# A new order for the first nine units of an attention and mixture-of-experts kernel

## The chip, the core and the metric

The kernel runs on one core of a Trainium2 chip, as one program. The metric is its time on the device in microseconds. The median of three runs of the kernel before is 1054.12 us (1052.29 to 1057.37).

## The reference

Attention over 8 batches and 12 heads, 448 tokens, 64 channels, in float32: q and k are normalized by the root of their mean square (and scaled by a gain for each channel), scores = q k^T / 8, softmax over the keys, times v. The heads of a token are put side by side to x (3584 tokens of 768). Then a mixture of eight experts: logits = x w_gate + a bias that depends on the token's modality; the expert with the largest logit takes the token, and the output is its softmax weight times relu(x w1) w2, with 768, 1024 and 768 channels.

## The kernel before, in words

Attention goes by units, 48 in all: a unit is two heads of one batch. A unit has seven steps (7 x 128 = 2 x 448 rows), so unit u starts at step n = 7u. At each step the program issues, in this order, `st` (the transposed scores of step j, lines 1009 to 1022, two products in a bank of their own, and ScalarE's exponential), then what the plan has for this step of the other stages, for units further ahead or behind.

What a unit goes through:

- `load` (line 826): q and k from HBM, one of six buffers each.
- `sumsq` (834): squares on ScalarE, summed over 64 channels by VectorE, or by GpSimd for the units that the plan's entry `ps` names.
- `rstd` (866): the roots, two activations (Ln, Exp) on ScalarE and five small instructions on GpSimd, for one to three units together.
- `norm` (884): q or k times its root, on GpSimd, for the very first q on VectorE.
- `tr` (898): four transposes on TensorE into a bank, then casts: `a0` the rounded part (`xw`), `a1` and `a2` its two halves into `w1w`, `dve` the rest that rounding left, a subtraction on VectorE. Moves by DMA from SP's queue put halves on the other partitions.
- `sa` (977): the scores once more, with rows as partitions, only for their maxima; VectorE takes the maximum of each row (`at_hlw<-sa`). Two banks alternate.
- `mt` (996): a transpose of the seven columns of maxima, a copy on ScalarE and a DMA that puts them as one row (row 64) below the rest of q. The second product of `st` reads this row, so that the exponential gets scores less their maximum. For units 0 and 1 ScalarE issues this DMA itself.
- `st`, then `csum` (sums of the exponentials, GpSimd and VectorE), `av` (1048: attention times v, one bank for all units), `avcopy` (1065: copies the bank out, on ScalarE, as x transposed), `sums`, `gates`, `recips`, `xt`.

The order is written out by hand. The table `PLAN` (line 34) has offsets from 7u for the steady part and, under `first`, a step for each stage of the first units; `when` (1382) reads it. Steps from -22 to -1 are the ramp before the first score product. Each engine works through its own queue in the order of issue. `warm` (1330) issues filling products on TensorE, two instructions a call, as many as the plan's `warm` says for a step, and `warmn` more at each step below 0. Casts, copies and subtractions go into lists for later steps (`pre` for ScalarE and VectorE, `post`). From step 30 on the plan is the steady one but for a few entries. Routing runs in gaps of the attention; the experts' two products (`ph`, `py`) follow from about 550 us on.

Of the kernel before, what the change touches and what calls it, by code (L numbers as in the profile page):

```python
# [66 lines left out]
def kernel(  # L67
# [737 lines left out]
    if True:  # L805
# [92 lines left out]
        def tr(u, g):  # L898
# [66 lines left out]
            if nm == "k" and not own:  # L965
                at(pre["V"], state["n"] + 2, across)
# [29 lines left out]
        def mt(u):  # L996
            t = T[u]
            ps = ps_t.tile([128, 512], F32, tag="t", name=f"mt{u}")
# [416 lines left out]
        for n in range(P["start"], NJ * NU):  # L1415
# [309 lines left out]
```

## Time and profile before

| | us |
|---|---|
| median of three runs | 1054.12 |
| the profiled execution | 1054.4 |
| its span | 1052.6 |
| first score product of unit 0 | 27.78 |
| of unit 8 | 119.34 |

Share of busy time over the span: TensorE 97%, VectorE 71%, ScalarE 68%, GpSimd 68%. Times in the rows below count from the start of the span. A row of a timeline has start, duration, engine, line, operation, what is written and read, and in brackets how long the engine was idle before and what ended that. Most operations carry line 52 or 53, a helper's, so tiles tell them apart: `at_hlw<-sa` is a maximum of rows, `xrw<-r` a square or a norm, `xw<-tr` a first cast, `w1w<-tr,xw` and `xw<-tr,gs,xw` the subtractions, `at_hhw<-av` a copy of x.

### The profile page before, as it was taken

What the parts mean: (1) busy time and instruction counts of PE and PEld (TensorE: products, weight loads), DVE (VectorE), ACT (ScalarE), POOL (GpSimd) and SP (SyncE); (2) the same over time, 40 slices, a digit from 0 to 9 for tenths busy, and PEclk for the clock granted to TensorE, in tenths of its full rate; (3) what the DMA queues carried; (4) which work ended last, traced back from release to release, by engine and by line L of the source; (5) the groups of instructions that cost most, each with busy time, mean ns of one, the idle gap of its engine ahead of it and who ended that gap; (6) DMA issues with size and microseconds to landing.
All of it is one profiled execution on the core that took longest, in us unless ns stands there. A gap on an engine that the chain in (4) does not pass through costs nothing.

```text
span 1052.6 us, 18833 instructions
## 1 busy us (share of the span) xinstructions
PE 1025.4 (97%) x6444; PEld 816.7 (78%) x6444; DVE 742.7 (71%) x1252; ACT 714.9 (68%) x1389; POOL 715.2 (68%) x752
## 2 busy tenths in 40 slices
PE   8899999999999999999999999999999999999996
PEld 7655656666566565655658999999999999999995
DVE  6666788878888878787676886756675567556740
ACT  6887998889898898987764655545564555545531
POOL 7788777897788887788966646865545554565451
PEclk9899999999999999999999999999999999999998
DMA  7756666867677766765566605233372432234161
GB/s 193 177 126 151 148 148 163 191 156 163 133 189 162 155 158 138 180 130 125 146 205 248 136 16 166 76 106 120 115 287 81 120 106 78 78 103 121 60 210 66
DMA packets 147961, 148.21 MB, mean 141 GB/s; under 512 B 72762, under 2 KB 137742, under 8 KB 147344
## 3 DMA queue, kind: packets, MB, share of 16 engines
q1 hardware_dynamic: 122458, 105.08, 41.3%
q0 software_dynamic: 25328, 41.82, 12.4%
q8 instruction: 53, 0.87, 0.4%
q14 instruction: 52, 0.43, 0.2%
q10 hardware_dynamic: 70, 0.02, 0.0%
HBM read 150.31 MB, written 33.39 MB: 175 GB/s over the span
## 4 chain that ended last, share of the span: by engine, by line
PE 84%; DVE 5%; DMA 3%; POOL 3%; ACT 2%; issue 2%; ACTq 0%; SPq 0%; POOLq 0%; DVEq 0%
PE ph L606 23%; PE py L636 21%; PE st L1016 12%; PE av L1058 9%; PE sa L988 4%; PE tr L906 3%; PE av L1054 2%; PE xt L1121 2%; PE sm L1077 2%; DVE at_hlw L52 2%; DMA w1w<-xw 1%; PE warm L1332 1%; PE sm L1084 1%; PE sa L983 1%; POOL r2w L52 1%
## 5 line engine op out<-in xcount | busy, mean ns | idle before, releaser
L606 PE MATMUL ph<-xw,w1w 128*128 128x256 f32 x2016 | 246.5, 283 | 2.2 <-ACT at_w2lw L52 1.1
L606 PEld LDWEIGHTS ph<-xw,w1w 128*128 128x128 f32 x2016 | 244.0, 192 | 4.2 <-ACT at_w2lw L52 1.2
L52 DVE TENSOR_REDUCE at_hlw<-sa 128x1 f32<-128x448 f32 x336 | 205.7, 619 | 43.5 <-PE sa L988 21.6
L1016 PE MATMUL st<-w1w 128*128 128x448 f32 (+1 forms) x480 | 183.2, 431 | 1.7 <-ACT r2w L52 1.1
L52 POOL DMA_INDIRECT r<-in_moe_w_dram,tb_w x60 | 82.7, 1379 | 53.0 <-DVE w1w L52 37.4
L52 ACT ACTIVATE r2w<-st 128x448 f32<-128x448 f32 x168 | 91.0, 545 | 36.8 <-PE st L1016 27.6
L52 ACT ACTIVATE hhw<-ph 128x512 fp32r<-128x512 f32 x56 | 33.5, 598 | 120.7 <-PE ph L606 120.7
L52 POOL TENSOR_TENSOR r2w<-r2w 128x448 f32<-128x448 f32 (+1 forms) x72 | 83.7, 1162 | 44.7 <-DVE r2w L52 26.5
L636 PE MATMUL py<-w2lw,hhw 128*128 128x384 f32 x448 | 113.7, 334 | 0.0
L988 PE MATMUL sa<-w1w 128*128 128x448 f32 (+1 forms) x288 | 109.2, 380 | 4.4 <-DVE at_hlw L52 2.6
L1016 PEld LDWEIGHTS st<-w1w 128*128 128x128 f32 (+1 forms) x480 | 85.9, 191 | 34.8 <-ACT r2w L52 8.5
L52 DVE TENSOR_TENSOR w1w<-r,w1w 128x768 fp32r<-128x768 f32 x112 | 103.2, 950 | 11.4 <-ACT w1w L52 10.2
L52 POOL DMA_INDIRECT r2w<-in_moe_w_dram,tb_vi x48 | 49.6, 1034 | 87.3 <-DVE w2lw L52 78.6
L52 ACT CAST w1w<-xw 64x448 fp32r<-64x448 f32 x188 | 105.7, 562 | 3.6 <-issue 1.4
L52 DVE TENSOR_TENSOR w2lw<-r2w,w2ha 128x1536 fp32r<-128x1536 f32 x28 | 49.1, 1757 | 81.6 <-ACT w2ha L52 81.6
L1016 PE MATMUL st<-w1w,w2ha 65*128 65x448 f32 x288 | 101.3, 372 | 0.0
L52 POOL TENSOR_TENSOR xrw<-r,at_hlw 112x512 f32<-112x512 f32 x95 | 97.7, 1049 | 1.0 <-PE tr L906 0.4
L52 ACT ACTIVATE at_w2lw<-st 128x448 f32<-128x448 f32 x168 | 90.6, 546 | 9.3 <-PE st L1016 4.5
L52 ACT CAST w1w<-r 128x768 fp32r<-128x768 f32 x112 | 95.1, 903 | 0.1
L52 ACT ACTIVATE yw<-py,ltn 128x384 f32<-128x384 f32 x55 | 29.4, 580 | 79.1 <-PE py L636 75.6
L636 PEld LDWEIGHTS py<-w2lw,hhw 128*128 128x128 f32 x448 | 80.9, 188 | 0.0
L52 POOL TENSOR_TENSOR r2w<-r2w,at_w2lw 64x448 f32<-64x448 f32 (+1 forms) x48 | 55.2, 1150 | 19.0 <-DVE r2w L52 9.2
(298 smaller groups left out, 2210.1 us busy)
## 6 DMA issues: line engine op xcount, KB each, us to landing
w1w<-xw SPq DMA_DIRECT2D x216, 112.0 KB
xg<-xrw SPq DMA_DIRECT2D x14, 768.0 KB
xrw<-xg SPq DMA_DIRECT2D x56, 192.0 KB
r<-in_q_dram SPq DMA_DIRECT2D x19, 448.0 KB
r<-in_k_dram SPq DMA_DIRECT2D x19, 448.0 KB
w2ha<-xw SPq DMA_DIRECT2D x72, 112.0 KB
w1w<-w1w SPq DMA_DIRECT2D x48, 112.0 KB
r2w<-in_v_dram SPq DMA_DIRECT2D x24, 224.0 KB
```

The costliest lines, as they stand in the source:

```text
L52: return fn(*a, **kw)
L606: PE.matmul(ps[:, i], lhsT=lt_, rhs=rt_[:, c], start=n == 0, stop=n == 17)
L636: PE.matmul(ps[n][:, :384], lhsT=lt_[:, j, 128 * t : 128 * t + 128], rhs=rt_[:, 384 * n : 384 * n + 384], start=j == 0 and m == 0, stop=j ...
L906: PE.transpose(sp[:, c], src[:, c], idn[:CP, :CP])
L983: PE.matmul(ps[:, :S], lhsT=qm_b[u % 2], rhs=hi_b[u % 2][1], start=True, stop=True)
L988: PE.matmul(ps[:, :S], lhsT=t["qq"][r, h, a : a + 128], rhs=t["kk"][h][r], start=True, stop=True)
L1016: PE.matmul(ps[:, :S], lhsT=l, rhs=t["qq"][:, h] if first else t["ql"][0:65, h], start=first and (j != 3 or h == 0), stop=not first and (j ...
L1054: PE.matmul(t["av"][:, :S], lhsT=vd_b[u % 2], rhs=t["p"][:, 3], start=False, stop=True)
L1058: PE.matmul(t["av"][64 * h : 64 * h + 64, :S], lhsT=vv[:, u % 3, j], rhs=t["p"][:, j], start=c == 0, stop=False)
L1077: PE.matmul(R[g][32 * i : 32 * i + 32, :S], lhsT=sel[:, m], rhs=T[u + i // 2]["cs"][:, i % 2], start=m == 0, stop=False, tile_position=(0, ...
L1084: PE.matmul(sm[32 * i : 32 * i + 32, :S], lhsT=wg[:, (4 * g + i) % NP], rhs=T[4 * g + i]["xt"], start=False, stop=True, tile_position=(0, ...
L1121: PE.transpose(ps[:CP, 128 * c : 128 * c + 128], T[u]["xt"][:, c * CP : (c + 1) * CP], idn)
```

## The change

- `PLAN` gets new steps for the first units. Ahead of step 0 remain units 0 and 1 up to their transposes (unit 1's `sa` not), the squares of unit 2 and 3, and unit 2's norms. Unit 1's `sa` go into steps 1 to 4 and its `mt` into 5; unit 2's `sa` into 6 to 10, `mt` 11; unit 3's into 11 to 16, `mt` 17; `sas` lists these steps one by one. Squares, norms and transposes of units 3 to 8 come later than before.
- The roots of the first units are taken one unit at a time (`rs` with `rs0`): units 0, 1, 2, 3 each by itself, then 4 and 5 together; before it was 0, then 1 and 2, then 3 to 5.
- Filling products: 12 and not 19 calls at the first step; other counts behind it, and now also at steps 0 to 7.
- The order of the casts is a table (`casts`), by default as before; for units 0 and 1 they are spread over more steps.
- GpSimd sums the squares of two transfers only; the q of units 2 and 3 goes to VectorE.
- The transpose of unit 0's maxima uses a bank of `st` in place of one of the transposes'.
- `avcopy` is a copy by VectorE for units 0 to 7.
- The gains are loaded behind two units and not three, and multiplied after the first norm; loads of units 6 to 10 and of the first v have other steps.

```diff
-'first': {... ('sq', 2): -18, ('sk', 2): -18, ('nk', 1): -16, ('nq', 1): -13, ... ('sa', 1): -5, ('mt', 0): -8, ('tk', 2): -8, ('tq', 2): -3, ... ('tq', 3): 5, ('mt', 1): 2, ... ('mt', 2): 8, ... ('sa', 2): 1, ('sa', 3): 9, ('sa', 4): 16, ('tq', 4): 12 ...}
-'rs0': {0: 0, 2: 1, 5: 0, 7: 0, 8: 2}, 'sastep': 1
-'warm': {-22: 19, -21: 3, -20: 1, -16: 4, -15: 1, -13: 5, -10: 2, -7: 3, -6: 1, -5: 1, 5: 1, 7: 1}
-'ps': [(6, 1), (4, 0), (3, 0), (2, 0)]
+'first': {... ('sk', 2): -18, ('sq', 2): -9, ... ('nk', 1): -17, ('nq', 1): -16, ... ('mt', 0): -8, ... ('tk', 2): 2, ('tq', 2): 3, ('mt', 1): 5, ('mt', 2): 11, ... ('tk', 3): 7, ('tq', 3): 9, ('mt', 3): 17, ... ('tq', 4): 15, ('sa', 4): 17 ...}
+'rs0': {0: 0, 1: 1, 2: 2, 3: 0, 5: 1, 7: 0, 8: 2}
+'warm': {-22: 12, -21: 3, -20: 1, -16: 5, -14: 1, -12: 1, -7: 3, -6: 2, -5: 1, -4: 1, -3: 1, 0: 2, 1: 2, 2: 1, 3: 1, 4: 2, 5: 2, 6: 2, 7: 1}
+'ps': [(6, 1), (4, 0)]
+'sas': {1: (1, 1, 2, 2, 3, 3, 4), 2: (6, 7, 8, 8, 9, 9, 10), 3: (11, 12, 13, 14, 15, 15, 16)}
+'casts': {(0, 1): (3, 4, 1, 4), (0, 0): (5, 5, 1, 4), (1, 1): (1, 5, 1, 2), (1, 0): (1, 4, 4, 5)}, 'vcopy': 8
...
-            ps = ps_t.tile([128, 512], F32, tag="t", name=f"mt{u}")
+            ps = (ps_t if u else ps_s).tile([128, 512], F32, tag="t" if u else "s", name=f"mt{u}")
...
-            A.copy(t["xt"], t["av"][:, :S])
+            if u < PLAN["vcopy"]:
+                V.tensor_copy(out=t["xt"], in_=t["av"][:, :S])
+            else:
+                A.copy(t["xt"], t["av"][:, :S])
...
-        for u in range(3):
+        for u in range(2):
             load(u)
         load_gains()
...
-                if a[0] < P["early"]:
-                    at(pre["A"], n + 1, a1)
-                    at(pre["A"], n + 1, a2)
-                    at(pre["A"], n + P["late0"], a0)
-                    at(pre["V"], n + P["late0"], d_)
-                    continue
-                at(pre["A"], n + 1, a0)
-                at(pre["V"], n + 1, d_)
-                at(post, n + 1, a1)
-                at(pre["A"], n + 2, a2)
+                c = P["casts"].get(a, CASTS)
+                at(pre["A"], n + c[0], a0)
+                at(pre["V"], n + c[1], d_)
+                at(pre["A"] if a[0] < P["early"] else post, n + c[2], a1)
+                at(pre["A"], n + c[3], a2)
```

## Rows read from the trace of the kernel before

**Rows 1.** The page, busy time of each engine over the whole span:

```profile
PE 1025.4 (97%) x6444; PEld 816.7 (78%) x6444; DVE 742.7 (71%) x1252; ACT 714.9 (68%) x1389; POOL 715.2 (68%) x752
```

**Rows 2.** Busy time by stretch: width, engines, granted clock, DMA share, GB/s:

```profile
27.78:39.51 11.73, 10.11 (x40) 7.94 (x39) 7.15 (x12) 8.28 (x19) 9.62 (x12) 0.71 0.73 178
39.51:49.68 10.17, 9.25 (x48) 5.67 (x47) 7.36 (x12) 9.71 (x24) 7.28 (x11) 1.00 0.60 149
49.68:85.88 36.20, 32.05 (x157) 18.11 (x155) 23.79 (x40) 30.65 (x75) 30.72 (x56) 1.00 0.67 152
85.88:119.34 33.46, 32.42 (x168) 19.43 (x169) 24.96 (x46) 28.51 (x67) 26.66 (x29) 1.00 0.55 123
119.34:205.96 86.62, 85.82 (x466) 52.75 (x465) 70.32 (x140) 77.09 (x178) 67.91 (x74) 1.00 0.70 164
28.60:31.50 2.90, 1.77 (x9) 1.08 (x8) 2.71 (x5) 2.83 (x7) 2.82 (x4) 1.00 0.87 219
31.50:38.30 6.80, 6.30 (x18) 5.40 (x19) 3.63 (x7) 3.50 (x9) 5.32 (x6) 0.50 0.77 176
```

**Rows 3.** Timeline of the ramp, single instructions and runs of one kind:

```profile
1.50 9.42 PE L1332 MATMUL warm<-idn,ones 128*128 128x128 f32 x56 [1.50 <-POOL idn masks.py:199]
8.00 1.04 POOL L52 TENSOR_TENSOR xrw<-r,at_hlw 112x512 f32<-112x512 f32 x1
...
19.93 2.31 POOL L52 TENSOR_TENSOR xrw<-xrw 112x256 f32<-112x256 f32 x5
...
23.32 0.28 PE L999 MATMUL mt<-idn,at_hlw 128*7 128x128 f32 x1 [0.20 <-DVE at_hlw L52]
23.43 1.73 PE L1332 MATMUL warm<-idn,ones 128*128 128x128 f32 x14
...
24.54 1.32 ACTq L52 DMA_DIRECT2D w1w<-xw  x1
...
28.18 0.44 PE L1016 MATMUL st<-w1w,w2ha 65*128 65x448 f32 x1
```

**Rows 4.** VectorE's groups from 15.5 to 23.3 us, by form:

```profile
L52 DVE TENSOR_REDUCE at_hlw<-sa 128x1 f32<-128x448 f32 x7 | 4.0, 613 | 0.0
L52 DVE TENSOR_REDUCE at_hlw<-xrw 112x8 f32<-112x512 f32 x3 | 2.0, 679 | 0.0
L52 DVE TENSOR_TENSOR w1w<-tr,xw 128x448 fp32r<-128x448 f32 x2 | 1.2, 618 | 0.4 <-ACT xw L52 0.4
```

**Rows 5.** The chain of waits, 27.8 to 32.0 us: start, duration, what:

```profile
27.84 0.54 ACT xw L52
...
28.61 3.15 DMA w1w<-xw
...
32.00 0.71 PE sa L988
```

**Rows 6.** TensorE's waits from 27.7 to 119.4 us: total, times, longest:

```profile
PE mt L999 <- DVE at_hlw L52: 1.8, 3, 0.9
PE av L1058 <- ACT at_hhw L52: 1.6, 2, 0.9
...
PE sm L1077 <- POOL at_hhw L52: 1.1, 1, 1.1
```

**Rows 7.** ScalarE's groups by form: units 8 to 15, then 26 to 28 us:

```profile
L52 ACT CAST w1w<-xw 64x448 fp32r<-64x448 f32 x32 | 18.0, 562 | 0.4
L52 ACT ACTIVATE at_w2lw<-st 128x448 f32<-128x448 f32 x29 | 15.8, 546 | 1.2 <-PE st L1016 0.5
...
L52 ACT ACTIVATE xrw<-r 112x512 f32<-112x512 f32 x17 | 10.7, 631 | 0.2
L52 ACT ACTIVATE xw<-tr,gs 128x448 fp32r<-128x448 f32 x8 | 5.1, 632 | 0.0
...
L52 ACT COPY at_hhw<-av 128x448 f32<-128x448 f32 x3 | 1.5, 516 | 0.0
L53 ACT ACTIVATE at_hlw<-at_hlw,lnb 112x48 f32<-112x48 f32 x2 | 0.7, 334 | 0.1
```

More of the change, by code (lines that the diff above doesn't have):

```diff
@@ new lines @@
+PLAN = {'rtj': 6, 'rushat': 36, 'av': (1, 1, 4, 6), 'xt': 4, 'xte': (2, 5), 'sm': 2, 'la': 6, 'rc': 9, 'csv': (1,), 'csj': (3, 6), 'csd': (1, 1), 'cse': (2, 1), 'sa': 14, 'mt': 6, 'tk': 21, 'tq': 18, 'nq': 26, 'nk': 26, 'sk': 49, 'sq': 50, 'rs': 48, 'ld': 58, 'first': {('sq', 0): -22, ('sk', 0): -21, ('nk', 0): -20, ('nq', 0): -18, ('sq', 1): -19, ('sk', 1): -19, ('sk', 2): -18, ('sq', 2): -9, ('rs', 0): -20, ('rs', 1): -18, ('rs', 2): -7, ('tk', 0): -18, ('tq', 0): -17, ('nk', 1): -17, ('nq', 1): -16, ('tk', 1): -13, ('tq', 1): -11, ('sa', 0): -15, ('mt', 0): -8, ('nk', 2): -5, ('nq', 2): -3, ('tk', 2): 2, ('tq', 2): 3, ('mt', 1): 5, ('mt', 2): 11, ('sk', 3): -6, ('sq', 3): -4, ('rs', 3): 1, ('nk', 3): 3, ('nq', 3): 3, ('tk', 3): 7, ('tq', 3): 9, ('mt', 3): 17, ('sk', 4): 2, ('sq', 4): 3, ('sk', 5): 5, ('sq', 5): 6, ('rs', 5): 8, ('nk', 4): 10, ('nq', 4): 11, ('tk', 4): 13, ('tq', 4): 15, ('sa', 4): 17, ('mt', 4): 24, ('nk', 5): 13, ('nq', 5): 14, ('tk', 5): 18, ('tq', 5): 21, ('sa', 5): 24, ('mt', 5): 31, ('sk', 6): 9, ('sq', 6): 10, ('sk', 7): 13, ('sq', 7): 14, ('rs', 7): 17, ('nk', 6): 19, ('nq', 6): 20, ('tk', 6): 23, ('tq', 6): 25, ('sa', 6): 30, ('mt', 6): 37, ('nk', 7): 23, ('nq', 7): 25, ('tk', 7): 29, ('tq', 7): 31, ('sa', 7): 37, ('mt', 7): 45, ('sk', 8): 16, ('sq', 8): 18, ('rs', 8): 30, ('nq', 8): 35, ('mt', 8): 50, ('sk', 9): 24, ('sq', 9): 23, ('nq', 9): 31, ('tk', 9): 43, ('ld', 6): -6, ('ld', 7): -4, ('ld', 8): 0, ('ld', 9): 6, ('ld', 10): 16}, 'rs0': {0: 0, 1: 1, 2: 2, 3: 0, 5: 1, 7: 0, 8: 2}, 'start': -22, 'warm': {-22: 12, -21: 3, -20: 1, -16: 5, -14: 1, -12: 1, -7: 3, -6: 2, -5: 1, -4: 1, -3: 1, 0: 2, 1: 2, 2: 1, 3: 1, 4: 2, 5: 2, 6: 2, 7: 1}, 'warmn': 1, 'early': 1, 'pmp0': 2, 'ramp': 10, 'pmp': (0, 0, 1, 1, 1, 0, 1), 'nv': [(0, 0)], 'pmpa': (1, 0, 1, 0, 1, 1, 1), 'rush': (1, 1, 1), 'ps': [(6, 1), (4, 0)], 'pa': [], 'rtr': 6, 'sml': 4, 'lv': (-4, 0), 'lg': 16, 'lz': 13, 'gc': 24, 's1': (1, 4), 'sas': {1: (1, 1, 2, 2, 3, 3, 4), 2: (6, 7, 8, 8, 9, 9, 10), 3: (11, 12, 13, 14, 15, 15, 16)}, 'casts': {(0, 1): (3, 4, 1, 4), (0, 0): (5, 5, 1, 4), (1, 1): (1, 5, 1, 2), (1, 0): (1, 4, 4, 5)}, 'vcopy': 8}
@@ L35 @@
+CASTS = (1, 1, 1, 2)
 MANUAL = {ET.PE, ET.DVE, ET.Activation, ET.Pool, ET.SP}
@@ L965, in tr @@
             if nm == "k" and not own:
-                at(pre["V"], state["n"] + 2, across)
+                at(pre["V"], state["n"] + 1 + PLAN["casts"].get((u, g), CASTS)[1], across)
             return a0, a1, a2, dve
@@ L1335 @@
         A.preload_act_table_set("natural_log_exp_and_others")
-        for u in range(3):
+        for u in range(2):
             load(u)
         load_gains()
-        for u in range(3, 6):
+        for u in range(2, 6):
             load(u)
@@ L1482 @@
                 norm(*a, V if a in P["nv"] else G)
-                if a == (0, 0):
+                if a == (0, 1):
                     gain_product()
```

5 lines of the change are left out of this document (2 added, 3 removed).

## The prediction

> **What bounds the kernel now.** The page first: TensorE is busy for 1025.4 of 1052.6 us, 97% [rows 1], so what can still be won lies in stretches where it waits or multiplies for nothing. Then the busy time by stretch, cut at the first score product (line 1016) of a unit, seven steps to a unit [rows 2]. Units 8 to 15 take 86.62 us, 10.83 each, with TensorE busy for 85.82: there TensorE itself is the limit, and nothing in this change reaches them. Ahead of them lie 27.78 us before the first score product and 91.56 us for units 0 to 7 (11.73 + 10.17 + 36.20 + 33.46). In these eight units TensorE is busy for 83.8 us, ScalarE for 77.2 and GpSimd for 74.3, so they are limited by waits that go round between engines, and one row shows the clock granted at half, 0.50 from 31.5 to 38.3, after a stretch with TensorE busy for 1.77 of 2.90. What unit 8 starts earlier, all behind it starts earlier: the order from step 30 on is the same in both plans, and I carry a gain at unit 8 one to one to the end.
>
> **The start: 5.1 us earlier.** Filling products stand ahead of the first transposes: 56 instructions to 10.92, 168 ns each; GpSimd's first product, the normalized k, was ready at 9.04 [rows 3]. The new plan puts 42 there (seven calls of two instructions fewer), which end at 8.57, so the transposes start at about 9.15 and the first `sa` product at about 12.0, behind twelve more filling instructions at 124 ns (1.73 / 14) [rows 3]. Then VectorE decides: from 15.5 to 23.3 it does unit 0's seven row maxima (613 ns each) and, between them, three sums of squares (2.0 us) and subtractions, unit 1's among them [rows 4]. The squares of units 2 to 5 move behind and the roots of unit 1 no longer wait for unit 2's, so from the first to the last maximum only the seven (4.3) and unit 0's two subtractions (about 0.62 each) are left: 5.5 us from 12.6, and unit 0's row transpose (line 999) runs at about 18.3 and not 23.32. Another bank costs it nothing: it waited for VectorE, not for a bank; the bank keeps it from queueing behind unit 1's casts, which are now late. The gains' loads, now ahead of unit 2's on SP, and the other steps of v's and later loads I cost at nothing: the first norms and squares read units 0 and 1 alone, and unit 1's moves are not read until step 1. A load that waits on SP for the norm that frees its buffer would delay the moves behind it; that is in the bounds of the two waits below. From its copy's issue at 24.54 to the product that reads the row at 28.18 were 3.6 us [rows 3]; from an issue at 18.85 that makes 22.45. Filling behind the transpose is now 34 instructions (4.2 us), so the first score product comes at 22.7: -5.1. If VectorE's early work hides no more than the filling taken away, it is -2.4; were the row alone the limit, -5.4.
>
> **Unit 0: 2.6 us longer.** What was done before the first score product is now inside unit 0: all of unit 1's `sa` products (steps 1 to 4), unit 2's transposes (steps 2, 3), three squares, one root. ScalarE is the queue in which this stands. Behind the first row's copy and its issue (1.32 us of ScalarE's time [rows 3]) come the rest of unit 1's casts (about 1.6), a root's two activations (0.7) and two squares (0.63 each): free at about 23.6. From there to the copy of unit 1's row: six exponentials (546 ns), a root (0.7), three squares (1.9) and unit 2's casts (0.63 + 4 x 0.56 + 0.54 and two small ones, 3.9) [rows 5, 7]: 9.8 us, issue at 33.6, row there at 37.2. TensorE reaches unit 1 at about 33.9 (11.2 us for unit 0, ScalarE's pace) and waits 3 us, because the row's transpose stands two steps ahead of its reader, where before it stood five. Queued behind that product are all of TensorE's work, and ScalarE's exponentials behind it. So unit 0 takes 14.3 and not 11.73. Bounds: no wait (11.2, 0.5 less than before) and 3.5 more than before, if loads hold up the row's DMA too.
>
> **Unit 1: 2.6 us longer.** Unit 3's `sa` starts two steps behind unit 3's q transpose (steps 9 and 11); before there were four. The chain of waits shows what lies between: the cast at 27.84 (0.54), a move of 3.15 us to its landing, 0.24 to the product at 32.00 [rows 5], 4.2 us in all. In two steps TensorE has some 1.5 us of work of its own. Counted from unit 1's row, q's transpose ends 4.7 behind (the first eight products of `av` stand ahead of it), ScalarE is some 0.7 late, and 4.2 make 9.6; TensorE is at the product by 6.2. I take a wait of 2.6, below the difference of 3.4, since the 3.15 was measured with the DMA engines 0.87 busy and unit 1 of before had 0.60 [rows 2]; unit 1's row transpose for unit 2 stands behind the same product. TensorE's own work behind the row is about 10.1, a steady unit's 10.7 [rows 2] with one transpose and two `sa` more and without sums, gates and x: 12.7 with the wait, and not 10.17. Bounds of the wait: nothing and 3.4.
>
> The Trainium skill (DMA: Bandwidth & Descriptors, Anatomy of one DMA) puts the fixed cost of a DMA at about 2.0 us, most of it the receipt of the last write. By that both waits would be some 1.1 us shorter, an estimate from that page, and the sum 2.2 better; the move's 3.15 [rows 5] is what this kernel pays, so the row decides.
>
> **Units 2 to 4: 0.8 shorter.** Here the eight copies of x count. On ScalarE one is 516 ns [rows 7]; on VectorE no row shows it: between 0.52 (the same) and 0.68 (its slowest reduction of 512 columns [rows 4]); I take 0.61, its reduction of 448 columns from the same memory. ScalarE loses 0.5 a unit, VectorE gains 0.6, and what stands behind it there are the maxima that free the `sa` buffers. TensorE waited 1.6 us in all for that copy, the single bank of `av` being free only then, 1.8 for row maxima and 1.1 for GpSimd's sums [rows 6]. The first goes. GpSimd is relieved of two sums of squares (2.31 each [rows 3]; 0.68 each on VectorE) and gets two more roots, so its 1.1 goes by half. But unit 4's `sa` again starts two steps behind its transpose (about 1.7 of wait), and ScalarE gets five squares more (3.2), unit 2's k casts (1.8) and two roots (1.4) and loses 3.6 of copies: 80 us of work in the eight units. So 35.4 and not 36.2; bounds 34 (ScalarE without a wait) and 37.5.
>
> **Units 5 to 7: 0.9 shorter**, the copies' wait alone: 32.5; bounds 31.9 and 33.5.
>
> **The sum.** -5.1 + 2.6 + 2.6 - 0.8 - 0.9 = -1.6 us. The profiled execution took 1054.4 (span 1052.6), 0.3 above the median of 1054.1, so against either it is the same step: 1052.5.
>
> **Rivals.** (1) *The two waits don't come*, because ScalarE, not the landing, sets TensorE's pace at both places: unit 0 11.2, unit 1 10.2, the rest as above: 22.7 + 11.2 + 10.2 + 35.4 + 32.5 = 112.0 for unit 8, 7.3 earlier: 1047. For it: in units 2 to 4 ScalarE is busy for 30.65 of 36.20 [rows 2], and more lands on it. Against it: the gap that a move needs, 4.2 us, is more than two of TensorE's steps.
> (2) *Slower: the clock falls in the wait for unit 1's row and again in that for unit 3's move.* Place: behind steps 7 and 11. It decides if TensorE's share there is no better than the 61% after which the clock fell in the kernel before [rows 2]; filling of one or two calls stands in each of steps 0 to 7 against it, none behind. Price: in 6.8 us at half clock TensorE was busy for 6.3, so 3.1 of full-clock work is lost each time: one fall 1055.6, two 1058.7. That the clock is released by activity and held back without it is also what the Trainium skill says (TensorE: Matmul & The Clock Gate, Part 1); the trace agrees, with 0.50 in that stretch.
> (3) *VectorE becomes the wait*: copies and two more sums of squares (6.3 us) land between maxima, and the later row transposes wait for it as unit 0's did. Then units 2 to 7 gain nothing and lose about 1: 1055. For it: 1.8 us of such waits already [rows 6]; against it: it is busy for 23.79 of 36.20.
>
> **How the numbers follow.** Forecast 0.38 (1049.5 to 1055.5), first rival 0.36, second 0.15, third 0.11. About 0.5%, 5.3 us, is what a measurement of this kernel can tell from no change: below 1048.8 lie most of the first rival (0.32) and 0.05 of the forecast, 0.37; above 1059.4 the worse half of the second and a little of the third, 0.12; between them 0.51. The range of 8 in 10 reaches over the first rival down to 1043.5 (its units 2 to 7 at their lower bounds, 2.0 less, and its start) and to two falls of the clock: 1059.
>
> **What would show it.** Right: the first score product at about 22.7, the row transpose ahead of it at 18.3; ScalarE without idle time in unit 0; TensorE idle for some 3 us ahead of unit 1's second product until a DMA of the ACT queue lands, and again ahead of the first `sa` product of unit 3; no wait of `av` for a copy; unit 8 at about 117.7. Wrong: a first score product later than 25; unit 1 started by 35 (then the first rival); a granted clock of 0.50 behind either wait; `av` or row transposes waiting for VectorE more than 2 us in all; any difference of stages behind unit 8.

## The result and the profile after

The changed kernel takes 1066.2 us (median of six runs, 1062.9 to 1067.7), the kernel before in the same comparison 1054.6 (1052.3 to 1057.4): 1.011 times as long, 95% interval 1.009 to 1.0129. The forecast was 1052.5 with 1059.0 as its upper end. The profiled execution took 1066.56 us with a span of 1064.8. Line numbers of the changed kernel are one higher than before in the rows below, those of the filling products (1336) four higher.

The page after, busy time of each engine, to be set beside [rows 1]:

```profile
PE 1030.3 (97%) x6448; PEld 817.5 (77%) x6448; DVE 749.2 (70%) x1262; ACT 712.4 (67%) x1385; POOL 708.0 (66%) x750
```

No engine does noticeably more. The stretches after, cut as before at the first score product of a unit (unit 0; unit 1; units 2 to 4; 5 to 7; 8 to 15), then one stretch ahead of a fall of the clock and three at half clock, in the columns of [rows 2]:

```profile
23.10:36.14 13.04, 9.86 (x58) 7.49 (x57) 7.68 (x13) 11.31 (x27) 11.13 (x22) 1.00 0.81 205
36.14:55.20 19.06, 15.09 (x56) 9.04 (x54) 9.99 (x16) 11.33 (x25) 11.58 (x20) 0.73 0.41 105
55.20:95.97 40.77, 34.77 (x163) 19.03 (x161) 28.71 (x48) 31.73 (x77) 31.02 (x57) 0.96 0.61 136
95.97:128.94 32.97, 32.48 (x169) 19.46 (x169) 26.11 (x49) 27.43 (x64) 26.20 (x28) 1.00 0.53 126
128.94:215.56 86.62, 85.81 (x466) 52.79 (x465) 71.22 (x142) 76.43 (x176) 67.84 (x74) 1.00 0.73 164
33.00:37.78 4.78, 2.01 (x11) 1.35 (x11) 2.61 (x5) 3.42 (x9) 3.34 (x7) 1.00 0.73 185
37.78:44.61 6.83, 6.33 (x18) 3.26 (x18) 2.62 (x5) 3.27 (x7) 2.97 (x6) 0.50 0.45 110
51.44:54.85 3.41, 3.41 (x9) 2.29 (x8) 1.82 (x3) 1.98 (x4) 3.41 (x5) 0.50 0.32 93
71.92:75.33 3.41, 3.41 (x13) 1.75 (x13) 2.33 (x4) 3.15 (x8) 3.33 (x4) 0.50 0.52 106
```

Set against the terms of the forecast, in us (difference from before):

| | forecast | profiled |
|---|---|---|
| start | -5.1 | -4.7 (23.10) |
| unit 0 | +2.6 | +1.3 (13.04) |
| unit 1 | +2.6 | +8.9 (19.06) |
| units 2 to 4 | -0.8 | +4.6 (40.77) |
| units 5 to 7 | -0.9 | -0.5 (32.97) |
| unit 8's first score product | -1.6 | +9.6 (128.94) |

By this cut the wait for unit 1's row, which the forecast counted with unit 0 (some 3 of its 14.3 us), lies in unit 1, behind that unit's first product.

Units 8 to 15 take 86.62 as before, so what is lost at unit 8 is not won back there. The span is 12.2 longer; the 2.6 that are not in these 9.6 lie behind unit 15, most of them (2.1) in the stretch from unit 47 to the last `ph`. It takes 478.5 us before, 480.6 after, and between 477.7 and 480.6 in the experiments, whatever they change in the first units, so I don't count it as the change's.

Every instant of TensorE up to unit 8's first score product can be sorted, from its records, into its own work at full clock, filling products, what the work took longer at half clock (half of its time there), and idle time (us; where two records overlap, the later one counts):

| kernel | work | filling | lost to half clock | idle | sum |
|---|---|---|---|---|---|
| before | 87.2 | 18.4 | 3.0 | 10.7 | 119.3 |
| changed | 88.0 | 18.6 | 6.6 | 15.7 | 128.9 |

So the 9.6 are 5.0 of idle time and 3.6 of slow clock, and 1.0 of work and filling.

TensorE's waits after, 23 to 129 us: total, times, longest (before: [rows 6]):

```profile
PE st L1017 <- DMA w1w<-xw: 3.8, 2, 2.1
PE sa L989 <- DMA w1w<-xw: 3.5, 2, 2.3
PE sa L989 <- DVE at_hlw L53: 2.6, 3, 1.9
```

Most of this is waiting for what a DMA brings: 3.8 for rows of maxima and 3.5 for moved halves, where before there was one such wait, 0.50 at 32.00. The wait of attention's bank for the copy of x is gone. The four waits of units 0 and 1, for unit 1's maxima, for the move that unit 2's first `sa` product reads, for unit 1's row and for the move that unit 3's first `sa` product reads:

```profile
33.40 0.28 PE L1000 MATMUL mt<-idn,at_hlw 128*7 128x128 f32 x1 [1.11 <-DVE at_hlw L53]
35.72 0.44 PE L989 MATMUL sa<-w1w 128*128 128x448 f32 x1 [1.19 <-DMA w1w<-xw]
38.28 0.74 PE L1017 MATMUL st<-w1w,w2ha 65*128 65x448 f32 x1 [1.69 <-DMA w1w<-xw]
49.91 0.44 PE L989 MATMUL sa<-w1w 128*128 128x448 f32 x1 [2.28 <-DMA w1w<-xw]
```

The chain of waits tells what they wait for:

```profile
35.27 0.15 ACT xw L53
35.45 2.79 DMA w1w<-xw
...
47.60 2.17 DMA w1w<-xw
...
54.20 0.92 DVE r2w L53
...
55.21 0.95 issue
```

First the row of unit 1 (its copy ends at 35.42, its DMA takes 2.79, unit 1's second product starts at 38.28), then the move for unit 3's first `sa` product (49.91), then VectorE's queue for unit 3's sixth (from 54.20). Unit 3's own row is the fourth place. SP's queue shows why:

```profile
63.60 1.35 SPq L141 DMA_DIRECT2D wg<-in_moe_w_gate_dram  x2
65.00 0.61 SPq L143 DMA_DIRECT2D modr<-in_moe_modality_id_dram  x1
65.65 0.55 SPq L144 DMA_DIRECT2D bia<-n_moe_modality_bias_dram  x1
66.25 0.43 SPq L832 DMA_DIRECT2D r<-in_k_dram  x1
66.77 0.81 SPq L1005 DMA_DIRECT2D w1w<-xw  x1
```

Unit 3's transposed maxima left TensorE at 64.8, but four loads of the gates' tables (`lg`, step 16) and a load of k (step 17) stand ahead of the row on SP; it is issued at 66.77, and its reader starts at 71.17 after a wait of 2.15.

The ramp after (before: [rows 3]):

```profile
1.49 7.60 PE L1336 MATMUL warm<-idn,ones 128*128 128x128 f32 x42 [1.49 <-POOL idn masks.py:199]
...
19.28 0.28 PE L1000 MATMUL mt<-idn,at_hlw 128*7 128x128 f32 x1 [0.27 <-DVE at_hlw L53]
...
19.83 3.51 PE L1336 MATMUL warm<-idn,ones 128*128 128x128 f32 x30
23.10 0.45 PE L1017 MATMUL st<-w1w 128*128 128x448 f32 x1
```

### The profile page after: what moved, and what is told of

Read it like the earlier page. It is cut to its first block, busy times and chain, and to the rows that moved or that the text cites. A ratio compares the mean times of both kernels' runs of the same rounds, so it can differ in the third digit from the quotient of the medians.

```text
span 1064.8 us, 18847 instructions
## 1 busy us (share of the span) xinstructions
PE 1030.3 (97%) x6448; PEld 817.5 (77%) x6448; DVE 749.2 (70%) x1262; ACT 712.4 (67%) x1385; POOL 708.0 (66%) x750
## 4 chain that ended last, share of the span: by engine, by line
PE 78%; DVE 9%; ACT 4%; DMA 3%; issue 3%; POOL 1%; SPq 1%; ACTq 0%; POOLq 0%; DVEq 0%
PE ph L607 19%; PE py L637 19%; PE st L1017 12%; PE av L1059 10%; PE sa L989 5%; PE tr L907 3%; PE av L1055 2%; PE xt L1125 2%; DVE at_hlw L53 2%; PE sm L1081 2%; DMA w1w<-xw 1%; DVE w1w L53 1%; DVE w2lw L53 1%; PE sa L984 1%; DVE yw L53 1%
## 5 line engine op out<-in xcount | busy, mean ns | idle before, releaser
L53 DVE TENSOR_TENSOR w1w<-r,w1w 128x768 fp32r<-128x768 f32 x112 | 103.3, 953 | 11.3 <-ACT w1w L53 10.1
L53 ACT ACTIVATE at_w2lw<-st 128x448 f32<-128x448 f32 x168 | 90.8, 544 | 17.9 <-PE st L1017 12.0
L53 POOL TENSOR_TENSOR xrw<-r,at_hlw 112x512 f32<-112x512 f32 x95 | 97.6, 1047 | 0.6
L989 PEld LDWEIGHTS sa<-w1w 128*128 128x128 f32 (+1 forms) x288 | 55.3, 192 | 19.5 <-DVE at_hlw L53 7.1
```

The costliest lines, as they stand in the source:

```text
L53: return fn(*a, **kw)
L989: PE.matmul(ps[:, :S], lhsT=t["qq"][r, h, a : a + 128], rhs=t["kk"][h][r], start=True, stop=True)
```

## The experiments

All ratios are to the kernel before, run beside them. "Units" gives the lengths of units 0 to 4, in us, from the profiled execution (before: 11.7, 10.2, 12.0, 11.2, 13.0; changed: 13.0, 19.1, 13.1, 14.6, 13.0).

**1. Filling ahead of the four products that waited** (the changed kernel).

```diff
+FILL = {('sa', 2, 0): 4, ('st', 1, 0): 6, ('sa', 3, 0): 9, ('st', 3, 0): 8}
+def fill(ps, *what):
+    for _ in range(FILL.get(what, 0)):
+        PE.matmul(ps[:, :128], lhsT=ones, rhs=idn, start=True, stop=True)
```

> The changed kernel with filling products put into four of the places where TensorE waits: 4 ahead of unit 2's first sa product, 6 ahead of unit 1's first score product, 9 ahead of unit 3's first sa product, 8 ahead of unit 3's first score product. They go to the bank that the product behind them overwrites. Theory A (the clock): the changed kernel lost its time because the granted clock fell three times (0.50 from 37.8 to 44.6, 51.4 to 54.9 and 71.9 to 75.3), half of the 13.2 us that TensorE was busy there; the waits themselves are the smaller part. Then the clock stays at 1.00, unit 1 shrinks from 19.1 to about 13.5 and unit 3 from 14.6 to about 13, and the time is about 6 us below the changed kernel, 1060. Theory B (the waits and ScalarE's pace alone; the falls lie on top of waits): less than 2 us gained, 1064 to 1067, even where the clock stays up.

Measured: 1064.8 us, 1.0105 (1.0088 to 1.0122): the time is theory B's, the length of unit 1 theory A's. Units 14.4, 13.2, 18.2, 11.1, 15.7. Units 1 and 2, the first two rows of a view by stretch:

```profile
37.50:50.71 13.21, 12.57 (x73) 8.87 (x72) 8.03 (x14) 10.03 (x23) 9.69 (x17) 1.00 0.40 98
50.71:68.94 18.23, 14.30 (x74) 8.36 (x73) 12.50 (x18) 11.89 (x28) 11.17 (x16) 0.91 0.56 133
```

Unit 1 falls from 19.06 to 13.21 at a clock of 1.00, while unit 0, which holds ten of the filling products, grows from 13.04 to 14.38: 4.5 us less for both, close to the 4.9 that TensorE lost in unit 1 to half clock. But the loss turns up again, in units 2 and 4, where the clock now falls (55.4 and 89.6). VectorE and GpSimd in unit 2 of this kernel:

```profile
50.39 3.00 DVE L53 SCALAR_TENSOR_TENSOR r2w<-at_w2lw,half 128x448 f32<-128x448 f32 x1
53.32 0.61 DVE L53 COPY at_hhw<-av 128x448 f32<-128x448 f32 x1
53.85 0.67 DVE L53 SCALAR_TENSOR_TENSOR xw<-tr,gs,xw 128x448 fp32r<-128x448 f32 x1
54.44 0.67 DVE L53 TENSOR_REDUCE at_hlw<-xrw 112x8 f32<-112x512 f32 x1
55.04 0.61 DVE L53 TENSOR_REDUCE at_hlw<-sa 128x1 f32<-128x448 f32 x1
...
49.77 1.04 POOL L53 TENSOR_TENSOR xrw<-r,at_hlw 112x512 f32<-112x512 f32 x1
50.77 1.15 POOL L53 TENSOR_TENSOR at_w2lw<-r2w,at_w2lw 128x448 f32<-128x448 f32 x1
51.88 1.03 POOL L53 TENSOR_TENSOR xrw<-r,at_hlw 112x512 f32<-112x512 f32 x1
53.54 1.13 POOL L53 TENSOR_TENSOR r2w<-r2w,at_w2lw 128x448 f32<-128x448 f32 x1 [0.63 <-DVE r2w L53]
```

VectorE's addition of exponentials, 0.68 us elsewhere, takes 3.00 and ends 0.48 us behind the last of three GpSimd instructions in a row; a copy of x, a subtraction and a sum of squares stand between it and the maximum for which TensorE waits (3.5 us).

**2. Transposes of units 2 to 4 two steps earlier.**

```diff
-('tk', 2): 2, ('tq', 2): 3, ('tk', 3): 7, ('tq', 3): 9, ('tk', 4): 13, ('tq', 4): 15
+('tk', 2): 0, ('tq', 2): 1, ('tk', 3): 5, ('tq', 3): 7, ('tk', 4): 11, ('tq', 4): 13
```

> The changed kernel with the transposes of units 2, 3 and 4 two steps earlier (k and q), so that their sa products again start four to five steps behind them. All else stays. Both theories: the waits of sa for a move (1.2 and 2.3 us) go. Theory A: with the second of them goes the fall at 51.4, but the fall at 37.8, behind unit 1's row, stays: 4 us less, about 1062. Theory B: 3.5 us less and no change where the clock falls. A third possibility, that ScalarE's order is what counts (the casts, earlier now, delay the exponentials and the row of unit 1): no gain, 1066, and unit 0 longer than 13.0.

Measured: 1066.1, 1.0114 (1.0097 to 1.013). Units 14.1, 19.7, 11.3, 11.5, 18.2. Of what was expected the third possibility has the time and the longer unit 0, but not the reason alone: units 2 and 3 gain some 5 us together, the transposes themselves now wait for GpSimd's norms (5.4 us in two places), and unit 4 takes the gain back. A lead (the steps between a stage and the one that reads it) at one stage needs it at the stage ahead.

**3. The gates' tables loaded two steps later.**

```diff
-'lg': 16
+'lg': 18
```

> The changed kernel with the four loads of the gate's tables issued at step 18 and not 16, so that on SP they no longer stand ahead of the DMA of unit 3's row of maxima (issued at 66.8, landed for TensorE at 71.2, where TensorE had waited 2.15 us and the clock then fell for 3.4). If the row was late because of SP's queue: its issue comes at about 65, the wait of 2.15 and the fall behind it (1.7) go, unit 3 shrinks from 14.6 to about 11.5 and the time by 3, 1063. If unit 3 is bound by GpSimd (13.9 us busy of its 14.6, the gate's constants among them): the wait goes, but unit 3 stays above 14 and the time at 1066.

Measured: 1067.8, 1.0139 (1.0121 to 1.0157). Unit 3 takes 11.4 (11.2 before) and not 14.6, the row is issued at 65.21, and the fall of the clock behind it is gone: the row's delay was nearly all of unit 3's loss. Unit 4 takes 17.0 and not 13.0, and the expected 1063 is missed.

**4. The copies of x back on ScalarE.**

```diff
-'vcopy': 8
+'vcopy': 0
```

> The changed kernel with all copies of x on ScalarE as before; this part alone is undone. If the copies on VectorE cost what they were to save (sa waited 1.9 us for a maximum at 58.6, which stood behind a copy and its wait): unit 2 shrinks by 1 to 2 and the time is 1064 to 1065. If they are worth what I forecast: units 2 to 7 grow by 1.5 to 3, waits of av for ScalarE come back, 1068 to 1069.

Measured: 1065.8, 1.011 (1.0092 to 1.0127), between what the two outcomes had expected: the copies are not the cause. Units 13.5, 17.9, 13.0, 12.1, 16.4.

In all four unit 5 starts at 95.7 to 97.9 us (changed: 96.0), whatever came ahead. The next run asks what holds it.

**5. Filling, and GpSimd's constants for the gates at step 38.**

```diff
-'gc': 24
+'gc': 38
```

> The changed kernel with the filling products of the first experiment, and with GpSimd's constants for the gates (16 small instructions, 5.8 us in the profile, step 24) issued at step 38. Theory: behind unit 3 GpSimd's queue decides. In the kernel with filling alone GpSimd works without a gap from 65 to 87 us; the norm of unit 7's q ended at 82.5 behind the constants, a load on SP waited for it, and the moves of unit 6's halves stood behind that load, so unit 6's score products for maxima waited and the clock fell at 89.6. Without the constants that norm ends some 5.8 us earlier: unit 4 takes 13 us or less instead of 15.65, no fall at 89.6, unit 8 starts at about 125.3 instead of 128.1, and the time is about 1062 (1064.8 with filling alone). Rival: VectorE or ScalarE holds unit 5's start at 96 whatever GpSimd does: unit 4 stays above 15 us and the time at 1064.8.

Measured: 1064.0, 1.0073 (1.0052 to 1.0094). Units 14.9, 13.4, 18.4, 10.8, 13.0; unit 6 takes 14.2 and not 12.2. The chain in experiment 1: GpSimd's norm of unit 7, the load on SP that overwrites what it read, the moves behind that load, and unit 6's first product on TensorE (each from its engine's timeline; for the last link the profile names no releaser):

```profile
81.05 1.47 POOL L53 TENSOR_TENSOR xrw<-r,at_hlw 112x512 f32<-112x512 f32 x1
...
82.54 0.34 SPq L832 DMA_DIRECT2D r<-in_q_dram  x1
82.98 1.10 SPq L920 DMA_DIRECT2D w1w<-xw  x2
...
87.92 0.44 PE L996 MATMUL sa<-w1w 128*128 128x448 f32 x1 [2.41 <-issue]
```

Without the constants ahead of it:

```profile
78.46 1.03 POOL L53 TENSOR_TENSOR xrw<-r,at_hlw 112x512 f32<-112x512 f32 x1
...
81.20 0.54 SPq L832 DMA_DIRECT2D r<-in_q_dram  x1
```

Unit 4 comes out as the theory had it (12.96), without the wait, and unit 5 starts at 93.6. But unit 6, where the constants now are, gives 2.0 back, and unit 8 starts at 128.6, not at 125.3.

**6. The same, unit 5's norms three steps later** (in this kernel unit 5's q is normalized from data of a later load).

```diff
-('nk', 5): 13, ('nq', 5): 14, ('tk', 5): 18
+('nk', 5): 16, ('nq', 5): 17, ('tk', 5): 19
```

> The same, and the norms of unit 5 issued at steps 16 and 17 (before 13 and 14), its k transpose at 19 (before 18). With filling alone, VectorE's addition of exponentials (both inputs in SBUF, normally 0.68 us) took 3.00 us at 50.39 while GpSimd ran a norm, an addition and a norm without a gap, and ended when GpSimd ran dry; unit 3's score product for maxima then waited 3.5 us and the clock fell at 55.4. Theory: VectorE waits there for GpSimd to pause, so without unit 5's norms in that place the addition takes about 1 us or less, the wait goes, no fall at 55.4, unit 2 takes 13 to 14.5 us instead of 18.23; unit 8 at about 121.5, time about 1058. Rival: VectorE is late because of the eight copies of x and the sums of squares given to it: the addition may be short, but the wait for its maximum stays above 2 us and unit 2 above 16 us: about 1062.

Measured: 1064.0, 1.0079 (1.0045 to 1.0114). The bounds that the rival gave hold (wait above 2, unit 2 above 16), and half of the theory: one GpSimd instruction less in the run, and VectorE's addition falls by as much, and with it TensorE's wait, from 3.5 to 2.5; unit 2 17.2.

```profile
50.75 2.02 DVE L53 SCALAR_TENSOR_TENSOR r2w<-at_w2lw,half 128x448 f32<-128x448 f32 x1
```

**7 and 8. On the kernel before: the constants at step 38, and, by itself, the copies of x of units 0 to 7 on VectorE.**

```diff
-'gc': 24
+'gc': 38
...
-A.copy(t["xt"], t["av"][:, :S])
+(V.tensor_copy if u < 8 else A.copy)(out=t["xt"], in_=t["av"][:, :S])
```

> The kernel before with the gates' constants at step 38 instead of 24, nothing else. Theory of GpSimd's queue: there too the load on SP waited for unit 7's norm behind the constants (issue at 76.1), though with less behind it; unit 4 takes 11.5 to 12.5 us instead of 13.01, unit 8 starts 0.5 to 1.5 us earlier: 1053. Rival: GpSimd was never late enough in the kernel before: no difference, 1054.2; or the constants now delay sums at step 38: 1055.

> One part of the change alone: the kernel before with the copies of x of units 0 to 7 on VectorE. By the prediction's terms this is worth the wait of attention's bank for the copy, 1.6 us in units 2 to 7, so about 1052.5. Rival: VectorE's copies delay the maxima and give as much back or more: 1054.2 to 1055.5.

Measured: 0.9987 (0.9966 to 1.0007) and 0.9989 (0.9969 to 1.0009), no difference either. With the constants late unit 4 takes 11.4 for 13.0 and unit 6 14.2 for 12.2. With the copies on VectorE the bank's wait for the copy is 1.2 instead of 1.6: it changes its engine rather than goes. Both runs also show how much one profiled execution differs from another: neither changes anything ahead of step 0, yet the first score product comes at 29.17 and 28.99 (before: 27.78), the clock falls at 18.3 and not at 31.5, unit 0 takes 8.7 and not 11.7, and unit 1 starts at 37.8 and 37.7 (before: 39.5).

**9. On the kernel before: 12 filling calls at the first step and not 19.**

```diff
-'warm': {-22: 19, ...}
+'warm': {-22: 12, ...}
```

> One part alone on the kernel before: 12 filling calls and not 19 at the first step (14 instructions fewer), nothing else. If the filling at the start is what sets the first transposes, as the prediction's term for the start has it, the first score product comes up to 2.4 us earlier and unit 1 starts 1.5 to 2.4 us earlier: 1052 to 1053. Rival: the norms and casts behind it set the pace, or the clock falls in the ramp for want of filling, and unit 1 starts at 37.7 to 39.5 us as before: 1054 to 1055.

Measured: 0.9998 (0.9981 to 1.0014). The first score product comes 1.4 us earlier (26.38), as much as it came later in 7; the time does not show it.

**10. The changed kernel, unit 1's `sa` products and row transpose back at their steps.**

```diff
-('mt', 1): 5 ... 'sas': {1: (1, 1, 2, 2, 3, 3, 4), ...}
+('mt', 1): 2 ... 'sas': {1: (-5, -4, -3, -2, -1, 0, 1), ...}
```

> The changed kernel with one part undone: unit 1's score products for maxima at steps -5 to 1 and its row transpose at step 2, as in the kernel before (the change has them at 1 to 4 and 5). Theory: the row's lead is what was lost, so unit 1's second score product no longer waits for the row, the fall of the clock at 37.8 goes; the first score product comes 1.5 to 3 us later than 23.1, units 0 and 1 together take 25 to 28 us instead of 32.1, and unit 8 starts at 123 to 126.5 instead of 128.9: 1060 to 1064. Rival: the lead of unit 1's row is not it; the missing transposes and norms of units 2 and 3 are, so the wait moves to unit 2 or 3's first product for maxima, the clock falls there, and unit 8 stays above 127: 1064.5 or more.

Measured: 1068.8, 1.0141 (1.0106 to 1.0176): the rival's time, with unit 8 at 133.67. The casts and moves that those products read are still at the changed steps, so TensorE waits in the ramp (2.1 us for a cast), the clock falls at 25.9 and the first score product comes at 30.20. Waits for moves rise to 5.0. Unit 1's row was one of several short leads, and undoing one alone moves the wait, as the rival had it.

**11. Filling, unit 1's addition on GpSimd, the constants one a step from 27 on** (unit 1's second sum is made of the first head's exponentials here).

```diff
-if h in CSV:
+if h in CSV and u != 1:
...
-if n == P["gc"]: gate_consts()
+if n == P["gc"]: consts.extend(gate_consts())   # now a list of 17
+if consts: consts.pop(0)()
```

> The changed kernel with the filling of the first experiment, with unit 1's addition of exponentials on GpSimd in place of VectorE (1.1 us there, 0.68 us less on VectorE), and GpSimd's gate constants one instruction a step from step 27 on in place of all at 24. Theory: the addition was held up on VectorE by GpSimd's run of instructions (3.0 us for 0.68) and that wait made unit 2 long; without it the wait of unit 3's product for its maximum falls from 3.5 us to 1.2 or less, the clock does not fall at 55, unit 2 takes 13 to 15 us instead of 18.2; unit 4 takes 13, unit 6 12.2 (no 2 us given back, as with all constants at step 38); unit 8 at 121.5 to 123.5, time 1056.5 to 1059. Rival: VectorE is late there by its own load (the copy of x, two sums of squares): wait above 2 us, unit 2 above 16.5, unit 8 above 125.

Measured: 1064.8, 1.0111 (1.0075 to 1.0147), not the time of the theory. The wait for VectorE falls to 1.3, near what was expected. In its place, in the same unit, unit 4's first `sa` product waits for its move, and unit 2 takes 20.2:

```profile
PE sa L996 <- DMA w1w<-xw: 4.1, 1, 4.1
PE sa L996 <- DVE at_hlw L53: 1.3, 1, 1.3
```

**12. The kernel before with the copies, more filling and the constants one a step.**

```diff
-'warm': {..., -13: 5, ...}, 'gc': 24
+'warm': {..., -13: 7, -12: 1, -11: 1, 0: 2, 1: 2, 2: 1, ...}, 'gc': 27   # one a step
```

> The kernel before with what the runs so far point to: copies of x of units 0 to 7 on VectorE, the gate constants one instruction a step from step 27 on, and more filling where its clock fell (two calls more at step -13, one each at -12 and -11, two at 0 and 1, one at 2). Theory: unit 4 takes 11.5 instead of 13.0 and unit 6 stays at 12.2 (the constants all at step 38 gave 1.6 back there), and the 3.0 us lost at half clock in the ramp or in unit 0 is saved, less about 1 us for the filling: unit 8 at 114.5 to 116.5 instead of 117.3 to 119.3, time 1050.5 to 1052.5. Rival: the filling costs what the clock gives, or another wait takes the place: 1053.5 to 1055.

Measured: 1053.3, 0.9983 (0.9964 to 1.0001): no difference, and the rival's other wait. Unit 4 gains (11.4), but a transpose in unit 5 waits 2.4 us for a norm among the constants and the clock falls at 91.0.

**13. The decisive one: the kernel before with TensorE's steps of the changed kernel for units 1 to 4, and nothing else** but the norms of units 4 and 5, which need a free buffer.

```diff
-('tk', 2): -8, ('tq', 2): -3, ('tk', 3): 0, ('tq', 3): 5, ('tk', 4): 8, ('tq', 4): 12, ('mt', 1): 2, ('mt', 2): 8, ('mt', 3): 16, ('mt', 4): 23, ('sa', 4): 16
+('tk', 2): 2, ('tq', 2): 3, ('tk', 3): 7, ('tq', 3): 9, ('tk', 4): 13, ('tq', 4): 15, ('mt', 1): 5, ('mt', 2): 11, ('mt', 3): 17, ('mt', 4): 24, ('sa', 4): 17
+('nk', 4): 2, ('nq', 4): 3, ('nk', 5): 7, ('nq', 5): 9, 'sas': as in the changed kernel
```

> The kernel before with the changed kernel's steps for TensorE's stages of units 1 to 4 alone (transposes, score products for maxima, row transposes), and the norms of units 4 and 5 as early as their buffers then allow; squares, roots, other norms, filling, casts and copies as before. Theory (the short leads of TensorE's stages are the cause): the first score product at 24 to 27.8, a wait for a row or a move of 2 us or more in unit 1 or 2 with the clock at half behind it, units 0 to 4 some 7 to 10 us longer together than in the kernel before, unit 8 at 125 to 129 and the time 1060 to 1066. Rival (the later squares, roots and norms are the cause): with the old ones nothing is late, units 0 to 4 at most 4 us longer, time 1053 to 1058.

Measured: 1062.9 us, 1.0076 (1.0051 to 1.0101). First score product at 25.17, units 11.9, 19.0, 12.7, 11.5, 12.9 (9.8 longer together than before), unit 8 at 126.52: all within what the theory gave, two of the waits a little under its 2 us. TensorE's longer waits of this kernel, then its unit 1 and its half clock:

```profile
33.92 0.28 PE L999 MATMUL mt<-idn,at_hlw 128*7 128x128 f32 x1 [1.14 <-DVE at_hlw L52]
36.27 0.71 PE L988 MATMUL sa<-w1w 128*128 128x448 f32 x1 [1.66 <-DMA w1w<-xw]
39.68 0.74 PE L1016 MATMUL st<-w1w,w2ha 65*128 65x448 f32 x1 [1.90 <-DMA w1w<-xw]
50.73 0.44 PE L988 MATMUL sa<-w1w 128*128 128x448 f32 x1 [1.96 <-DMA w1w<-xw]
```

```profile
37.07:56.02 18.95, 15.10 (x55) 9.12 (x54) 9.51 (x17) 11.10 (x24) 9.84 (x14) 0.69 0.46 117
35.30:45.50 10.20, 7.33 (x22) 4.31 (x22) 4.78 (x8) 4.96 (x10) 6.34 (x10) 0.50 0.54 136
```

The same four products wait as in the changed kernel, about as long (there 1.11, 1.19, 1.69 and 2.28), and unit 1 takes 18.95 for 19.06, though the clock falls one wait earlier here. 0.76% (0.51 to 1.01) of the 1.1% is there. Unit 3's loss is not: the row stands behind the same loads on SP, is issued at 67.87, and its reader at 69.80 has waited for 0.36. So the loads alone do not make that loss.

**14 and 15. The other half: the changed kernel with squares, roots and norms of units 0 to 5 at the steps of before (norms of 4 and 5 as in 13), without and with the filling of experiment 1.**

```diff
-('sq', 2): -9, ('nk', 2): -5, ('nq', 2): -3, ... 'rs0': {0: 0, 1: 1, 2: 2, 3: 0, 5: 1, ...}, 'ps': [(6, 1), (4, 0)]
+('sq', 2): -18, ('nk', 2): -14, ('nq', 2): -8, ... 'rs0': {0: 0, 2: 1, 5: 0, ...}, 'ps': [(6, 1), (4, 0), (3, 0), (2, 0)]
```

> The changed kernel with the squares, roots and norms of units 0 to 5 at the steps of the kernel before (and two sums of squares back on GpSimd), the norms of units 4 and 5 as early as their buffers allow; TensorE's stages as changed. Theory (short leads of TensorE's stages): the start is later by 1 to 3 us since more lies ahead of it on VectorE and ScalarE, the waits for the row of unit 1 and for unit 3's move stay, the clock falls in unit 1 again, and the time is 1063 or more. Rival (the later squares, roots and norms): units 2 to 4 take 36 us instead of 40.8 and the falls go: 1058 or less.

> The same with the filling products of the first experiment ahead of the four products that waited. Theory (short leads): the clock is held in unit 1, unit 1 takes 13.2 instead of 19, and with the norms early nothing upstream is late in units 2 to 4, so unit 8 is at 122 to 125 and the time 1057 to 1061: the waits are filled, not gone. Rival (the later norms were the cause): filling only adds its own length, 1 to 2 us, to the kernel without it.

Measured: 1065.4, 1.0098 (1.0068 to 1.0127), and 1066.2, 1.0111 (1.0071 to 1.0151). Earlier norms do not mend it, and 14's time is the theory's: units 2 to 4 take 40.2, not 36, and the move for unit 3 is waited for as before (2.26) with the half clock behind it. The start goes to 31.0 and 29.1, with the clock at half in the ramp; with the later start the wait for unit 1's row goes, against the theory. 15 misses its 1057 to 1061: with units 1 to 3 at 12.6, 14.6 and 10.7, unit 4 takes 17.2, so the filling gains nothing over 14.

**16. The kernel before with 12 filling calls, the copies on VectorE, and filling where its clock fell.**

```diff
-'warm': {-22: 19, ..., -13: 5, ...}
+'warm': {-22: 12, ..., -13: 7, -12: 1, -11: 1, 0: 2, 1: 2, 2: 1, ...}
```

> The kernel before with the parts of the change that gave time back to nobody: 12 filling calls at the first step and not 19, copies of x of units 0 to 7 on VectorE; and filling where its clock fell (two calls more at step -13, one each at -12 and -11, two at 0 and 1, one at 2). TensorE's stages keep their leads. Theory: start at 26 to 26.5, no loss at half clock, unit 8 at 114.5 to 116, time 1050 to 1052, 0.3% faster than before. Rival: the filling costs what the clock and the start give: 1053 to 1054.5, no difference.

Measured: 0.9989 (0.997 to 1.0008). The profile records no half clock ahead of unit 8, and unit 8 at 117.07, 2.3 earlier (2.1 in 8); the time does not tell it from the kernel before: the rival. No version was clearly faster than the kernel before.

## Why the prediction was wrong

**Start, right, with errors that cancel.** The row transpose is at 19.28 (18.3 was forecast) and its row's DMA is issued at 20.90 (18.85), but from there to its reader at 23.60 are 2.7 us and not 3.6, and the filling behind the transpose is over at 23.34. The first score product comes at 23.10 (22.7). One reading was wrong: the 168 ns for a filling product is a mean over two paces. In the trace they follow each other every 0.21 us up to 7.6 us (7.1 after) and every 0.11 behind that; the fourteen that were left out are of the faster kind, so the first filling ends at 9.09 and not at 8.57.

**Unit 0, too short by 1.8, not too long by 1.3.** Of the 14.3 us some 3 were the wait for unit 1's row. That wait stands ahead of unit 1's second product, so by the prediction's own cut it belongs to unit 1, and unit 0 was forecast at 11.2, ScalarE's pace without a gap. It took 13.04 with ScalarE busy for 11.31. TensorE waited in it 1.11 us for VectorE's maxima ahead of unit 1's row transpose and 1.19 for the move that unit 2's first `sa` product reads; the forecast had neither.

**Unit 1: here the forecast failed.** The step is "Unit 1: 2.6 us longer". Both waits came where the prediction put them, and shorter: 1.69 for the row (3, counted with unit 0), 2.28 for unit 3's move (2.6). TensorE's own work, 10.22, is what was forecast (10.1). The term put at nothing what follows a wait. TensorE was busy for 2.01 of the 4.78 us ahead of 37.78, 42% (1.77 of 2.90, 61%, ahead of the fall before [rows 2]); then the granted clock was 0.50, the lower of the two levels (1.2 GHz), for 6.83, and again for 3.41 behind the second wait. Its 6.33 + 3.41 of work there would have taken half as long at the upper level: 4.9 us lost. With the row's wait and the move's these make the unit: 10.22 + 1.69 + 2.28 + 4.87 = 19.06. This was the second rival, place and mechanism, which got 0.15; but its price, 1058.7 for two falls, is far from 1066, since it had neither the 5.4 of units 2 to 4 nor the 2.6 behind unit 15. The plan showed how little stands against a fall: one or two filling calls in each of steps 0 to 7, 2.1 us over unit 0's 13, while each wait is some 2 us, and none ahead of the second wait. Experiment 1 confirms it: with filling ahead of the waits the clock stays at 1.00 and unit 1 takes 13.21. Experiment 13 shows where the waits come from: TensorE's steps on the kernel before, with the norms of units 4 and 5, which are read only from step 13 on, make all four, and 8.0 of the 11.6 us. The other 3.6 were not taken apart by a run of their own.

**Units 2 to 4: the second failure, 5.4 us.** The step is "Units 2 to 4: 0.8 shorter". The term was a sum of engine loads, and no engine was full. What decided were two queues. One is SP, whose loads were costed at nothing but for the bounds of two waits: the row of unit 3 stands behind the gates' loads, TensorE waits for 2.15 and loses 1.7 at half clock behind it (3.2 by experiment 3). The other is VectorE's, whose addition waits for GpSimd (1.86 of TensorE's time in the changed kernel, 3.5 when unit 1 is filled). Unit 4 takes 13.0 as before; GpSimd's constants for the gates show there only when the units ahead get shorter (2.7 between experiments 1 and 5), and on the kernel before (1.6 by experiment 7). These gains don't add up, and this was the largest surprise: experiments 1, 2, 3 and 15 shorten one or two units by 3 to 6 us and get it back in a later one. In 1, 2 and 3 unit 5 starts at nearly the same time; that a unit which starts earlier finds the next queue just as late is shown for GpSimd's constants by 5, and argued for the others. The third rival, VectorE as the wait, is true in one place only (1.86 us).

**Units 5 to 7, the copies.** -0.5 for -0.9. A copy on VectorE takes 0.612 us (0.61 was taken), but alone it is worth nothing that can be measured (experiment 8): what the bank waits for is then VectorE.

**The carry** of unit 8's delay held through unit 15: units 8 to 15 are the same to 0.01 us. Behind them lie 2.6 more, which are not shown to be the change's. With the measured lengths in place of its terms, cut as the table cuts them, the sum is 1052.5 + 6.3 (unit 1) + 5.4 (units 2 to 4) - 1.3 (unit 0) + 0.4 (start) + 0.4 (units 5 to 7) + 2.6 (behind unit 15) = 1066.3, against 1066.56 profiled. That is bookkeeping; the causes rest on the experiments. The lower end of the range, 1043.5, does not come out of what it names (1047 less 2.0 and 0.3 is 1044.7), which changes nothing here.

Left open: what the earlier start is worth with the leads kept. Experiments 9 and 16 bring unit 8 forward by 2.3 us in the profile, but in 7 and 8, with the ramp left as it was, unit 1 starts 1.7 and 1.9 us earlier too. The medians show no difference.

## What to carry to other kernels

Work moved behind the start of a pipeline that goes round between engines is not paid by its length but by the lead that its readers lose: count, for every product, the steps between the stage it reads and itself, against cast, move and row (4.2 us here [rows 5]), and where the lead is shorter, lengthen it or fill it. Put the half clock behind such a wait into the sum from the start: here 4.9 us for two waits of 1.69 and 2.28, though none for the 1.86 at 58.55. And do not trust a gain in one unit until a later fixed point, here unit 8's start, has moved by more than it differs between executions (some 2 us here).

## What the hardware showed that was not expected

VectorE's addition of exponentials, two operands in SBUF, takes 0.68 us when GpSimd is idle and up to 3.04 beside it. This is so in the kernel before too: 21 of its 48 additions take 0.76 to 2.55 us, and every one of these ends 0.48 to 0.49 us behind the end of a GpSimd instruction. VectorE's subtractions, which read one operand from a bank of TensorE, take 0.62 to 0.69 beside GpSimd as elsewhere. Which engine goes first when both are ready differs. At 54.20 in the changed kernel, at 50.39 in experiment 1 and at 50.75 in experiment 6 (2.04, 3.00 and 2.02 us) the addition ended only behind the last of two or three GpSimd instructions that followed each other without a gap, and these kept their usual 1.0 to 1.15. Their data are not the reason: the last of them is a norm of another unit (twice) or the other head's sum. But the other order stands in the traces too, here in the kernel before: VectorE got in behind the first of two, though the second followed without a gap, and GpSimd's second, a norm, took 1.42 us in place of 1.04:

```profile
62.51 1.31 DVE L52 SCALAR_TENSOR_TENSOR r2w<-r2w,half 128x448 f32<-128x448 f32 x1
...
62.20 1.14 POOL L52 TENSOR_TENSOR at_w2hb<-r2w 128x448 f32<-128x448 f32 x1
63.30 1.42 POOL L52 TENSOR_TENSOR xrw<-r,at_hlw 112x512 f32<-112x512 f32 x1
```

The Trainium skill (SBUF — State Buffer, "SBUF: two separate sides") says that VectorE with two inputs in SBUF and a GpSimd instruction that reads SBUF share a pair of ports as an exclusive lock, held for a whole instruction. The rows agree in both directions, and add that VectorE can come second several times in a row. What decides that is open. That it is the port, and not another cause, was not tested by itself; with the addition gone (experiment 11) the wait shrank with it.

A row's DMA, 896 numbers, landed 2.79 us after its issue on ScalarE's queue (at 35.45) and 4.35 after its issue on SP's (66.77), but in experiment 13 in less than 2 on SP's (67.87 to 69.80); the move at 47.60, 32 times as many bytes, took 2.17. So neither size nor queue alone set the time.
